# Splitting and joining the weights of an attention and MoE kernel another way, with an order read from a table

## The chip, the core and the metric

The kernel runs on one core of a Trainium2 chip. The metric is the device time of one execution in microseconds (us). The core has TensorE (PE in the profile; PEld is its weight loads), VectorE (DVE), ScalarE (ACT), GpSimd (POOL) and SyncE (SP), which here issues all the transfers. SBUF is the working memory; PSUM holds what TensorE writes, in banks of 128 x 512 float32.

## The reference, cut to what matters

```python
scores = scale * q @ k^T                 # 4 batches, 8 heads, 576 x 576, head size 64
mask   = scores >= 32nd largest of its row
attn   = softmax over the masked row;  x = attn @ v          # x: 2304 x 512
h = x @ w_in;  g = h * sigmoid(1.702 * h);  x = g @ w_out    # 512 -> 2048 -> 512
a = x @ w1;  b = x @ w2;  out = ((a * b) @ w3) @ w_out2      # 512 -> 1024 -> 1024 -> 512
```

The five weight matrices arrive as float64, q, k, v and x's path as float32. In the kernel w_out2 is called w4.

## The kernel before, in words

The 2304 rows are 18 tiles of 128. A tile runs through eight heads (`head`), `tile_end` (the 512 columns of x, scaled) and `moe`. A head is one score product `S` (L904, four matmuls of 288 columns; in tiles 4 and 13, which lie across two batches, eight), then on VectorE four MAX8 (L926) and three MATCH_REPLACE8 (L929) that find the 32nd largest of each row, then on ScalarE `cut` (L944), `exp` (L947) and `a hi` (L953), on GpSimd `a lo` (L956, L957), a DMA transpose, and for each pair of heads `av` (L971, 18 matmuls, or 36).

Every float32 factor of a product is cut into two float16 halves, hi and lo, and a product of 512 columns is three matmuls for each block of 128 rows (L668, L669, L670: hi by hi, hi by lo, lo by hi). `product_op` issues it as two operations of six matmuls, called half products here. A tile's `moe` has 28 of them: 8 `h`, 8 `x2`, 4 `a`, 4 `b` and 4 `o`, 504 in all; 32 more multiply w3 by w4 once (`w34`).

The weights are 72 blocks of 128 x 512: 8 of w4, 16 each of w3, w_in, w_out and of w1 and w2 together (`w12`). Each block goes through `load64`: a DMA of 512 KB into a raw buffer; `w low` on ScalarE (L513) and `w sign` on GpSimd or ScalarE (L518, L523), which put parts of the float32 word into the block; `w main` on ScalarE (L527), which rewrites the high words in the raw buffer; and `w join` on VectorE (L531), which joins the raw buffer's words to the block and frees the raw buffer. `l2_scale` then sums squares (`gram` on TensorE, L558) and works out one power-of-two scale `sc` for each matrix. `split_pe` makes the halves of a block: a float32 product with the identity brings it into a PSUM bank (`w in`, L595, two matmul records), ScalarE writes hi from the bank (`w hi`, L598), and VectorE writes lo as bank times scale less hi (`w lo`, L601). All 72 blocks go this way.

The four banks called `mm` serve all of these products; two larger pairs (`sp`) hold scores.

The order of the instructions on each engine is made before anything runs. The class `Order` holds every operation with the engines that may run it (`alts`), what it depends on and which buffers it takes (`acq`) and frees (`rel`); `run` goes forward in its own clock and gives each free engine, of the operations that could go, the one of least `prio`. In the kernel before, `prio` is a due time plus a shift that `later` reads from a table by the operation's name and due time, and where more than one engine may run an operation, the first that is free takes it, with waits from `LONGER`. The engines then run their lists strictly in order, and wait for each other by semaphores.

Of the kernel before, what the change touches and what calls it, by code (L numbers as in the profile page):

```python
# [19 lines left out]
P = 128  # L20
# [11 lines left out]
class Op:  # L32
    __slots__ = ("alts", "fn", "prio", "acq", "rel", "left", "users", "ready", "end", "eng", "lat", "tag", "seq", "done", "start", "why", "data")


class Order:
# [8 lines left out]
    def __init__(self):  # L45
        self.ops = []
        self.pools = {}
        self.both = set()

# [9 lines left out]
    def op(self, alts, due, deps=(), env=None, acq=(), rel=(), tag="", lat=None, data=0.6):  # L59
# [15 lines left out]
    def run(self, log=None):  # L75
# [13 lines left out]
        while n < len(self.ops):  # L89
# [18 lines left out]
            for e in engs:  # L108
# [65 lines left out]
PEP = ("w4", "w3", "win", "wout", "w12")  # L174
# [4 lines left out]
TIMES = (-20, 60, 130, 220, 330, 500, 750, 1000)  # L179
LATER = {  # L180
# [12 lines left out]
    'cut': (-16.5, -12.5, -10, 2.5, 54.5, -57, -110, -124),  # L193
    'diag': (36.5, -1.5, -37.5, -60, -103.5, -26, -28, -5.5),
    'diag sum': (77, 52, 49.5, 66, 118, 98, 82.5, 95),
    'esc': (-38.5, -52.5, -90.5, -104, -69, -58.5, -19.5, -46.5),
    'exp': (7, 5.5, -23.5, -30, -30, -23, 28, 80.5),
# [4 lines left out]
    'gram': (-18.5, 62.5, 143, 136, 220.5, 192.5, 75.5, 27),  # L202
# [72 lines left out]
}  # L275

def later(tag, due):

    v = LATER.get(tag)
    if v is None:  # L280
# [1019 lines left out]
```

## Time and profile before

| | |
|---|---|
| three runs, us | 1081.84, 1083.23, 1085.87 |
| median of the runs | 1083.23 us |
| span of the profiled execution, first to last instruction | 1081.3 us |
| TensorE busy | 990.1 us, 92% |
| VectorE busy | 932.2 us, 86% |
| ScalarE, GpSimd busy | 821.4 us (76%), 768.7 us (71%) |
| mean granted TensorE clock | 0.96 |

For the profiled execution only the span is given, no time of its own around it; the median lies 1.9 us above it. Busy is the time in which at least one instruction of the engine runs, so neighbours that overlap count once. A matmul's recorded length is longer than its turn on the engine: what a matmul costs in a full row is the distance from its start to the next start.

### The profile page before, as it was taken

The numbers are of one execution on the slowest core, as the hardware profiler recorded it, in microseconds if no ns is written. First come the engines' busy times: TensorE is split into PE (matmuls) and PEld (weight loads), VectorE is DVE, ScalarE is ACT, GpSimd is POOL, SyncE is SP. The second block draws the span as 40 slices with busy tenths as digits, with TensorE's granted clock in tenths as the row PEclk, the third lists the DMA queues.
The fourth block names the chain that finished last, engine by engine and source line by source line (L and its number), as shares of the span: only waits on it lengthen the run. The fifth ranks groups of instructions, "written<-read, shape, count | busy, mean of one in ns | idle before, by whom it ended". The sixth has DMA issues, their size and how long they took to land.

```text
span 1081.3 us, 18734 instructions
## 1 busy us (share of the span) xinstructions
PE 990.1 (92%) x5816; PEld 508.2 (47%) x5816; DVE 932.2 (86%) x2098; ACT 821.4 (76%) x1570; POOL 768.7 (71%) x1096
## 2 busy tenths in 40 slices
PE   4658899588899989999999998999999999999997
PEld 2334444334444445455454554555455555555443
DVE  4889899799999899999999999999999999996111
ACT  7878779888876778879788787778887887767432
POOL 4555545847757879879889878869799797767321
PEclk7779999699999999999999999999999999999999
DMA  8979968869836847876868858867877876556222
GB/s 254 287 200 244 236 128 251 161 149 199 175 73 104 147 104 151 141 143 123 146 126 151 148 110 134 157 129 120 145 135 120 144 141 123 103 111 119 48 59 68
DMA packets 428739, 156.96 MB, mean 145 GB/s; under 512 B 406624, under 2 KB 414816, under 8 KB 428640
## 3 DMA queue, kind: packets, MB, share of 16 engines
q1 hardware_dynamic: 428640, 155.78, 71.1%
q8 instruction: 45, 0.74, 0.3%
q14 instruction: 54, 0.44, 0.1%
HBM read 52.43 MB, written 4.72 MB: 53 GB/s over the span
## 4 chain that ended last, share of the span: by engine, by line
PE 50%; DVE 16%; DMA 11%; POOL 10%; ACT 8%; issue 4%; SPq 0%; POOLq 0%; DVEq 0%; ACTq 0%
PE mm L668 13%; PE mm L669 13%; PE mm L670 13%; DVE m8s L926 6%; DVE wsb L929 5%; DMA tsb<-hsb 5%; PE mm L971 4%; PE s_ps L904 4%; POOL hlb L957 2%; POOL hsb L456 2%; PE mm L595 2%; DMA ats<-hlb 2%; DMA qts<-hsb 1%; DMA wout<-in_moe_w_in_dram 1%; DVE w L531 1%
## 5 line engine op out<-in xcount | busy, mean ns | idle before, releaser
L926 DVE MAX8 m8s<-wsb 128x8 f32<-128x576 f32 x432 | 323.7, 755 | 4.8
L929 DVE MATCH_REPLACE8 wsb<-m8s,wsb 128x576 f32<-128x576 f32 x288 | 214.1, 743 | 0.0
L957 POOL TENSOR_TENSOR hlb<-ysb,hlb 128x512 f16<-128x512 f32 x144 | 167.9, 1166 | 0.0
L668 PEld LDWEIGHTS <-tsb 128*128 128x128 f16 x1072 | 104.9, 98 | 133.1 <-DMA tsb<-hsb 21.5
L668 PE MATMUL mm<-w,tsb 128*128 128x512 f16 x432 | 163.9, 379 | 2.7 <-DMA tsb<-hsb 2.5
L670 PEld LDWEIGHTS <-tsb 128*128 128x128 f16 x1072 | 105.1, 98 | 127.2 <-issue 1.3
L670 PE MATMUL mm<-w,tsb 128*128 128x512 f16 x432 | 163.7, 379 | 0.0
L669 PE MATMUL mm<-w,tsb 128*128 128x512 f16 x432 | 163.7, 379 | 0.0
L669 PEld LDWEIGHTS <-tsb 128*128 128x128 f16 x1072 | 104.9, 98 | 111.3 <-issue 8.0
L668 PE MATMUL mm<-wout,tsb 128*128 128x512 f16 x352 | 133.6, 380 | 7.6 <-DMA tsb<-hsb 5.4
L944 ACT ACTIVATE s_ps<-s_ps,m8s 128x576 f32<-128x576 f32 x144 | 102.8, 714 | 42.2 <-DVE m8s L926 34.1
L670 PE MATMUL mm<-wout,tsb 128*128 128x512 f16 x352 | 133.6, 380 | 0.0
L669 PE MATMUL mm<-wout,tsb 128*128 128x512 f16 x352 | 133.6, 380 | 0.0
L947 ACT ACTIVATE ysb<-s_ps,nbs,asm 128x576 f32<-128x576 f32 x144 | 120.2, 835 | 10.3 <-DVE nbs L936 4.8
L926 DVE MAX8 m8s<-s_ps 128x8 f32<-128x576 f32 x144 | 109.1, 758 | 16.4 <-PE s_ps L904 14.9
L668 PE MATMUL mm<-win,tsb 128*128 128x512 f16 x288 | 110.2, 383 | 7.2 <-DMA tsb<-hsb 7.0
L904 PE MATMUL s_ps<-kts,qts 128*128 128x288 f16 (+1 forms) x640 | 99.6, 295 | 13.2 <-ACT ysb L947 12.1
L669 PE MATMUL mm<-win,tsb 128*128 128x512 f16 x288 | 110.1, 382 | 0.0
L670 PE MATMUL mm<-win,tsb 128*128 128x512 f16 x288 | 109.9, 382 | 0.0
L1120 POOL TENSOR_TENSOR fsb<-fsb 128x512 f32<-128x512 f32 x68 | 87.4, 1286 | 29.7 <-ACT fsb L1111 25.6
L929 DVE MATCH_REPLACE8 wsb<-m8s,s_ps 128x576 f32<-128x576 f32 x144 | 107.9, 749 | 0.0
L971 PE MATMUL mm<-v2s,ats 128*128 128x130 f16 (+1 forms) x1440 | 96.3, 225 | 10.5 <-DMA ats<-hlb 8.1
(171 smaller groups left out, 1875.8 us busy)
## 6 DMA issues: line engine op xcount, KB each, us to landing
w<-in_moe_w_dram SPq DMA_DIRECT2D x16, 512.0 KB, 6.9
wout<-in_moe_w_in_dram SPq DMA_DIRECT2D x16, 512.0 KB, 5.7
wout<-in_moe_w_out_dram SPq DMA_DIRECT2D x16, 512.0 KB, 4.7
qts<-qts SPq DMA_DIRECT2D x36, 128.0 KB, 2.5
out_dram<-fsb SPq DMA_DIRECT2D x18, 256.0 KB, 2.4
w<-in_moe_w_out_dram SPq DMA_DIRECT2D x8, 512.0 KB, 6.3
psb<-in_moe_w_dram SPq DMA_DIRECT2D x8, 512.0 KB, 5.3
tsb<-in_moe_w_dram SPq DMA_DIRECT2D x8, 512.0 KB, 4.1
```

What stands on the lines that cost most here:

```text
L456: nc.gpsimd.tensor_tensor(lo(), src(), hi(), op=ALU.subtract)
L668: nc.tensor.matmul(o, a[:, i, :], hi, start=(first and i == 0), stop=False)
L669: nc.tensor.matmul(o, a[:, i, :], lo, start=False, stop=False)
L670: nc.tensor.matmul(o, a[:, 4 + i, :], hi, start=False, stop=(last and i == 3))
L904: nc.tensor.matmul(E["sp"][r : r + n, i], qe[q_][:, h, r : r + n], kt[:, j, i * HS : (i + 1) * HS], start=k_ == 0, stop=k_ == 1,)
L926: nc.vector.max(out=E["m8"][:, 8 * i : 8 * i + 8], in_=E["sp"] if i == 0 else E["w"])
L929: nc.vector.match_replace(out=two(E["w"]) if i == 0 else E["w"], in_to_replace=E["m8"][:, 8 * i : 8 * i + 8], in_values=E["sp"] if i == 0 ...
L944: nc.scalar.activation(E["sp"], E["sp"], AF.Prelu, bias=E["m8"][:, TOPK - 1 : TOPK], scale=-1.0, alpha=1.0 / FAR)
L947: nc.scalar.activation(two(E["y"]), E["sp"], AF.Exp, bias=E["nb"], scale=nesc)
L957: nc.gpsimd.tensor_tensor(hl()[:, S + SR : 2 * S], E["y"][:, 0:SM], hl()[:, 0:SM], op=ALU.subtract)
L971: nc.tensor.matmul(heads_av()[r : r + n, j_], e["at"][:, i, r : r + n], v2[:, j_, blk, :], start=(i == 0), stop=(i == 8))
L1120: nc.gpsimd.tensor_tensor(E["f"], E["f"], E["f2"], op=ALU.mult)
```

## The change

- `w main` writes its result into a bank of `mm` and no longer into the raw buffer, which is free from then on; `w join` reads the bank.
- `l2_scale` can write a scaled identity, identity times minus `sc`, with GpSimd (`w turn`) into a quarter of a tile of `tsb`. It is written for w4, for w3, for w1 and for w2.
- For these 40 blocks `split_pe` is new: a float32 product with the scaled identity puts minus the scaled block into the bank; ScalarE writes hi, minus the bank; a product of the bfloat16 view of the identity with hi adds hi to the bank (`w less`); lo, minus the bank, is written by ScalarE (`A`) or VectorE (`V`).
- For the 32 blocks of w_in and w_out `split_back` takes its place: ScalarE writes hi from SBUF; a product of the bfloat16 identity with hi puts hi into a bank (`w back`); VectorE writes lo, block times scale less bank.
- `prio` and the engine of every operation come from a table, `PLAN`. It unpacks to one word for each of the 5232 operations, in the order in which the code creates them: the low 13 bits are a rank (each of 0 to 5231 stands once), the high bits the number of the engine in `alts`. `TIMES`, `LATER`, `LONGER` and `later` are gone.
- An operation may be held back until another one has gone in the order (`after`): the loads of k, and of v, one after the other, likewise `k T`, `a hi`, `a T`, and `x T` behind the last `g T` of two tiles before. The buffer of k's transpose is taken at the load, that of x at the first `av`. These say what `run` may choose; no waits for the chip are written by them alone.

Counted through the code, the table's words say: of the 72 `w lo`, 32 are those of `split_back` on VectorE, 30 of the others stand on ScalarE and 10 on VectorE; `w sign` stands 60 times on GpSimd and 12 times on ScalarE. The operations of rank 0 to 2070 hold, among others, all 72 blocks' joins and splits, all 32 `w34`, 47 `S` (heads 0 to 46 in order), 185 MAX8, 139 MATCH_REPLACE8, 20 `av` and 91 half products of `moe`. Outside the weights the lo and hi operations of these ranks that VectorE has are: 10 `kv lo`, 8 of them those of the first batch, which are VectorE's in both kernels, 3 `q lo`, one of them likewise, 3 `p lo`, 3 `g lo`, 8 `kvr lo`, 5 `kvr hi`, and 6 other hi; ScalarE has 12 of the `w sign`. The operations behind the last MAX8 (rank 5068) hold 50 half products.

```diff
-        o.alts, o.prio, o.lat, o.data = alts, due + later(tag, due), lat, data
-        if len(alts) > 1:
-            o.alts = [(e, c, f, max(w + LONGER.get((tag, e), 0.0), -1.0)) for e, c, f, w in alts]
+        o.after = after
+        rank, k = self.plan[len(self.ops)]
+        o.alts, o.prio, o.lat, o.data = [(*alts[k][:3], 0.0)], 0.2 * rank, lat, data
...
-                    if o.done or r > now:
+                    if o.done or r > now or (o.after is not None and not o.after.done):
...
+def plan():
+    words = array.array("H", zlib.decompress(base64.b85decode("".join(PLAN))))
+    return [(w & 8191, w >> 13) for w in words]
...
         def f_main():
-            high = words(E[raw_pool])
-            nc.scalar.activation(high, high, AF.Copy, scale=2.0 ** -112)
+            nc.scalar.activation(E["mm"], words(E[raw_pool]), AF.Copy, scale=2.0 ** -112)
 
         def f_join():
             d = dst.bitcast(U32)
             nc.vector.scalar_tensor_tensor(
-                d, words(E[raw_pool]).bitcast(U32), 3, d, op0=ALU.logical_shift_left, op1=ALU.bitwise_or
+                d, E["mm"].bitcast(U32), 3, d, op0=ALU.logical_shift_left, op1=ALU.bitwise_or
             )
...
-        mn = act(0.57, due, f_main, deps=[ld, sg], tag="w main")
-        return dve(0.65, due, od.two(f_join), deps=[sg, mn], env=E, rel=[raw_pool], tag="w join")
+        mn = act(0.57, due, f_main, deps=[ld, sg], env=E, acq=["mm"], rel=[raw_pool], tag="w main")
+        return dve(0.62, due, f_join, deps=[sg, mn], env=E, rel=["mm"], tag="w join")
...
+        def f_turn():
+            nc.gpsimd.tensor_scalar(turned, ident, sc, -1.0, op0=ALU.mult, op1=ALU.mult)
...
+    def split_back(hi, lo, src, sc, due, deps, env=None, acq=()):
...
+        def f_hi():
+            nc.scalar.activation(hi(), src(), AF.Copy, scale=sc)
+
+        def f_back():
+            nc.tensor.matmul(E["mm"], upper(ident), hi(), start=True, stop=True)
+
+        def f_lo():
+            nc.vector.scalar_tensor_tensor(lo(), src(), sc, E["mm"], op0=ALU.mult, op1=ALU.subtract)
...
+    def split_pe(hi, lo, src, scaled, due, deps, env=None, acq=()):
...
         def f_in():
-            nc.tensor.matmul(E["mm"], ident, src(), start=True, stop=True)
+            nc.tensor.matmul(E["mm"], turned, src(), start=True, stop=False, skip_group_check=True)
 
         def f_hi():
-            nc.scalar.activation(hi(), E["mm"], AF.Copy, scale=sc)
+            nc.scalar.activation(hi(), E["mm"], AF.Copy, scale=-1.0)
+
+        def f_less():
+            nc.tensor.matmul(E["mm"], upper(ident), hi(), start=False, stop=True, skip_group_check=True)
 
         def f_lo():
-            nc.vector.scalar_tensor_tensor(lo(), E["mm"], sc, hi(), op0=ALU.mult, op1=ALU.subtract)
...
+            nc.scalar.activation(lo(), E["mm"], AF.Copy, scale=-1.0)
+
+        def f_lo_v():
+            nc.vector.tensor_scalar(lo(), E["mm"], -1.0, None, op0=ALU.mult)
...
-        hi = act(0.58, due + 6, f_hi, deps=[y], env=E, acq=["hl"], tag="a hi")
+        hi = act(0.58, due + 6, f_hi, deps=[y], env=E, acq=["hl"], tag="a hi", after=last_of.get("a hi"))
```

## Rows read from the trace of the kernel before

**Rows 1.** Stretches: from:to, length, busy by engine, clock, DMA share, GB/s.

```profile
40.00:80.00 40.00, 23.84 (x111) 12.59 (x112) 35.61 (x83) 30.67 (x64) 20.31 (x34) 0.75 0.89 218
...
200.00:240.00 40.00, 27.79 (x131) 14.02 (x130) 37.02 (x75) 31.64 (x57) 20.83 (x29) 0.79 0.70 145
...
0.00:400.00 400.00, 323.23 (x1765) 162.46 (x1766) 354.33 (x759) 312.39 (x578) 243.79 (x365) 0.90 0.80 183
400.00:440.00 40.00, 37.92 (x248) 19.90 (x247) 38.24 (x92) 30.30 (x61) 35.69 (x53) 0.96 0.72 136
440.00:960.00 520.00, 513.56 (x3215) 270.96 (x3213) 499.22 (x1157) 422.64 (x827) 440.52 (x617) 1.00 0.73 134
960.00:1081.30 121.30, 115.39 (x594) 54.93 (x592) 40.46 (x93) 56.06 (x105) 48.67 (x63) 1.00 0.38 74
```

**Rows 2.** The chain that ended last: start, length, what; a float32 product.

```profile
143.48 0.86 PE mm L595 x2
```

**Rows 3.** Timeline, TensorE: start, length, engine, line, operation.

```profile
955.51 0.65 PE L904 MATMUL s_ps<-kts,qts 128*128 128x288 f16 x4
...
956.00 1.21 PE L971 MATMUL mm<-v2s,ats 128*128 128x130 f16 x18
...
957.05 0.38 PE L668 MATMUL mm<-w,tsb 128*128 128x512 f16 x1
...
957.27 0.38 PE L669 MATMUL mm<-w,tsb 128*128 128x512 f16 x1
```

**Rows 4.** TensorE's groups by line, 0 to 400 us: count, busy, mean ns, idle before.

```profile
L668 PE MATMUL mm<-wout,tsb 128*128 128x512 f16 x112 | 42.6, 380 | 6.3 <-DMA tsb<-hsb 4.1 <-DVE w L726 0.8 <-DVE hsb L601 0.6
L904 PE MATMUL s_ps<-kts,qts 128*128 128x288 f16 x140 | 26.8, 321 | 10.5 <-ACT ysb L947 9.5 <-DMA qts<-qts 0.8
L971 PE MATMUL mm<-v2s,ats 128*128 128x130 f16 x288 | 24.0, 241 | 8.3 <-DMA ats<-hlb 6.1 <-DVE w L726 1.4 <-DVE w L601 0.3
L668 PE MATMUL mm<-w,tsb 128*128 128x512 f16 x62 | 23.6, 380 | 0.2 <-DVE w L601 0.2
...
L668 PE MATMUL mm<-win,tsb 128*128 128x512 f16 x52 | 20.2, 388 | 4.5 <-DMA tsb<-hsb 4.5
...
L904 PE MATMUL s_ps<-kts,qts 128*64 128x288 f16 x64 | 5.7, 291 | 1.4 <-ACT ysb L947 1.4
L971 PE MATMUL mm<-v2s,ats 128*64 128x130 f16 x108 | 5.3, 228 | 0.0
```

**Rows 5.** Timeline, VectorE: the distance between starts; the last MAX8.

```profile
960.27 0.74 DVE L926 MAX8 m8s<-wsb 128x8 f32<-128x576 f32 x1
...
960.93 0.07 DVE L929 MATCH_VALUE_LOAD wsb<-m8s,s_ps 128x8 f32 x1
...
961.65 0.09 DVE L929 MATCH_VALUE_LOAD wsb<-m8s,wsb 128x8 f32 x1
...
990.07 0.76 DVE L926 MAX8 m8s<-wsb 128x8 f32<-128x576 f32 x1
```

**Rows 6.** VectorE's groups by line, 0 to 400 us.

```profile
L926 DVE MAX8 m8s<-wsb 128x8 f32<-128x576 f32 x127 | 94.8, 752 | 0.7
...
L926 DVE MAX8 m8s<-s_ps 128x8 f32<-128x576 f32 x43 | 32.6, 758 | 6.0 <-PE s_ps L904 5.2 <-ACT w L523 0.5
...
L531 DVE SCALAR_TENSOR_TENSOR w<-wout,w 128x512 uint32<-128x512 uint32 x32 | 26.5, 844 | 4.4 <-ACT wout L527 4.3
L601 DVE SCALAR_TENSOR_TENSOR wout<-mm,wsm,wout 128x512 f16<-128x512 f32 x24 | 17.4, 743 | 0.3
...
L726 DVE SCALAR_TENSOR_TENSOR w<-mm,w 128x512 f16<-128x512 f32 x8 | 5.5, 682 | 2.3 <-ACT w L723 2.3
```

**Rows 7.** All of L531 (joins) in one stretch, busy us.

```profile
sum 360.00, DVE 61.19; mean DVE 6.80
```

**Rows 8.** ScalarE's groups by line, 0 to 400 us: a read from a bank.

```profile
L598 ACT ACTIVATE wout<-mm,wsm 128x512 f16<-128x512 f32 x24 | 16.3, 685 | 5.3 <-PE mm L595 5.3
```

**Rows 9.** TensorE's waits, 0 to 400 us: for whom, us, times, longest.

```profile
PE s_ps L904 <- ACT ysb L947: 10.9, 8, 3.6
```

More of the change, by code (lines that the diff above doesn't have):

```diff
@@ L1 @@
+import array
+import base64
 import heapq
+import zlib
 from contextlib import ExitStack
@@ L32 @@
 class Op:
-    __slots__ = ("alts", "fn", "prio", "acq", "rel", "left", "users", "ready", "end", "eng", "lat", "tag", "seq", "done", "start", "why", "data")
+    __slots__ = ("alts", "fn", "prio", "acq", "rel", "left", "users", "ready", "end", "eng", "lat", "tag", "seq", "done", "start", "why", "data", "after")
 class Order:
@@ L173 @@
 PE_DUE, PE_OUT = 100.0, 20.0
[L174 removed]
+TURN = ("w4", "w3")
 SIGN_G = 0.5
[L179 to L180 removed]
[12 rows of a table removed]
[L193 to L197, printed above, removed]
[4 rows of a table removed]
[L202 removed]
[12 rows of a table removed]
[L215 removed]
[19 rows of a table removed]
[L235 to L238 removed]
[27 rows of a table removed]
[L266 removed]
@@ L545, in wcol, with l2_scale @@
         return wsm[:, ncol[0] - 1 : ncol[0]]
-    def l2_scale(blocks, deps):
+    def l2_scale(blocks, deps, turned=None, free=()):
         E = {}
@@ L587, in l2_scale @@
         c = dve_chain(due, f_scale, deps=[b], env=E, rel=["mm"], tag="w scale")
-        return inv, sc, c
-    def split_pe(hi, lo, src, sc, due, deps, env=None, acq=()):
+        if turned is None:
+            return inv, sc, c
+        return inv, (turned, pool(0.35, due - 40, f_turn, deps=[c] + list(free), tag="w turn")), c
+    def split_back(hi, lo, src, sc, due, deps, env=None, acq=()):
         E = {} if env is None else env
+        def f_hi():
[4 more added lines that the diff above has]
+            nc.vector.scalar_tensor_tensor(lo(), src(), sc, E["mm"], op0=ALU.mult, op1=ALU.subtract)
+        h = act(0.61, due - PE_OUT, f_hi, deps=deps, env=E, acq=acq, tag="w hi")
+        b = pe(0.24, due - PE_DUE, f_back, deps=[h], env=E, acq=["mm"], tag="w back")
+        return dve(0.66, due - PE_OUT, f_lo, deps=[b], env=E, rel=["mm"], tag="w lo")
@@ L600, in f_lo @@
         def f_lo():
-            nc.vector.scalar_tensor_tensor(lo(), E["mm"], sc, hi(), op0=ALU.mult, op1=ALU.subtract)
-        a = pe(0.87, due - PE_DUE, f_in, deps=deps, env=E, acq=["mm"] + list(acq), tag="w in")
-        h = act(0.58, due - PE_OUT, f_hi, deps=[a], tag="w hi")
-        return dve(0.66, due - PE_OUT, f_lo, deps=[h], env=E, rel=["mm"], tag="w lo")
-    def split_all(w, first, srcs, sc, deps, name):
-        if name not in PEP:
-            return [split_to(w, first + i, src, sc, deps) for i, src in enumerate(srcs)]
+            nc.scalar.activation(lo(), E["mm"], AF.Copy, scale=-1.0)
@@ new lines, in f_lo_v, with split_all @@
+        def f_lo_v():
+            nc.vector.tensor_scalar(lo(), E["mm"], -1.0, None, op0=ALU.mult)
+        a = pe(0.87, due - PE_DUE, f_in, deps=list(deps) + [ready_turned], env=E, acq=["mm"] + list(acq), tag="w in")
+        h = act(0.48, due - PE_OUT, f_hi, deps=[a], env=E, tag="w hi")
+        l = pe(0.24, due - PE_DUE, f_less, deps=[h], env=E, tag="w less")
+        return op([("A", 0.48, f_lo, 0.0), ("V", 0.6, f_lo_v, 1.0)], due - PE_OUT, deps=[l], env=E, rel=["mm"], tag="w lo")
+    def split_all(w, first, srcs, scaled, deps):
@@ L729, in weights @@
             ready["w34"].append(dve(0.66, due, f_lo34, deps=[h34], env=E, rel=["mm"], tag="w34 lo"))
-        ii, si, di = l2_scale([block(w12, i) for i in range(16)], cin)
-        ready["win"] = split_all(win, 0, [block(w12, i) for i in range(16)], si, [di] + sp3, "win")
+        ii, si, di = l2_scale([block(w12, i) for i in range(16)], cin, quarter(4, 2) if "win" in TURN else None)
+        ready["win"] = split_all(win, 0, [block(w12, i) for i in range(16)], si, [di] + sp3)
         cout = [
@@ L734, in weights @@
         ]
-        io, so, do = l2_scale([block(w12, i) for i in range(16)], cout)
-        ready["wout"] = split_all(wout, 0, [block(w12, i) for i in range(16)], so, [do] + cout + pr, "wout")
+        io, so, do = l2_scale([block(w12, i) for i in range(16)], cout, quarter(4, 3) if "wout" in TURN else None)
+        ready["wout"] = split_all(wout, 0, [block(w12, i) for i in range(16)], so, [do] + cout + pr)
         srcs = [rows(w, i, j) for w in (w1, w2) for j in range(NP_) for i in range(KB)]
@@ L818, in f_sum @@
             nc.tensor.matmul(E["mm"][:, 0:1], ones[0:SR], upper(ar)[0:SR], start=False, stop=True)
-        ld = dma(2.1 if is_v else 1.5, due - 6, f_load, env=E, acq=[sk, "rest"] + (["v2"] if is_v else ["h", "kr"]), tag="kv load", data=1.0)
+        ld = dma(
+            2.1 if is_v else 1.5, due - 6, f_load, env=E, acq=[sk, "rest"] + (["v2"] if is_v else ["h", "kr", "kt"]), tag="kv load",
+            data=1.0, after=last_of.get(("load", is_v)),
+        )
+        last_of["load", is_v] = ld
         a = act(0.93, due, f_abs, deps=[ld], tag="kv abs")
@@ L840, in f_t @@
             nc.sync.dma_start_transpose(out=E["kt"][:, :, SM:S], in_=E["kr"].rearrange("p h d -> p (h d)"))
-        kready[b, hp] = [dma(3.9, due, f_t, deps=[m, r], env=E, acq=["kt"], rel=["h", "kr"], tag="k T", data=1.1)]
+        last_of["k T"] = dma(
+            3.9, due, f_t, deps=[m, r], env=E, rel=["h", "kr"], tag="k T", data=1.1, after=last_of.get("k T")
+        )
+        kready[b, hp] = [last_of["k T"]]
     qready, qhold = {}, {}
@@ L1070, in tile_end @@
         )
-        X["xt"] = dma(1.32, due, f_t, deps=[s], env=X, acq=["t"], rel=["h"], tag="x T")
+        X["xt"] = dma(1.32, due, f_t, deps=[s], env=X, acq=["t"], rel=["h"], tag="x T", after=last_of.get(("g T", t - 2)))
     def hi_lo(due, E, src, deps, rel, acq=(), tag="", wait=2.0, wait_hi=2.0):
```

190 lines of the change are left out of this document (125 added, 65 removed), and 80 rows, old and new, of tables (LATER, LONGER).

## The prediction

> **What bounds the kernel now.** I read the stretches first, then the two timelines, then the groups by line, then the waits. The stretches cut the span in two. From 440 to 960 us TensorE is busy 513.6 of 520 us at a clock of 1.00, and from 960 to the end 115.4 of 121.3; before 400 us it is busy only 323.2 of 400, at a mean clock of 0.90 [rows 1]. So from 400 us on the end is set by how much TensorE work is still to be done, and before that TensorE has room. There VectorE is the fullest engine, 354.3 of 400 us, with ScalarE next, 312.4 [rows 1]; VectorE stays full, 499.2 of 520 us from 440 to 960, until its last MAX8 ends at 990.8, 90.5 us before the end [rows 1, 5]. A reader should take from this that a microsecond of TensorE work saved before 400 us is worth nothing by itself. It counts only if products of later stages move forward into the room, and these wait for VectorE: for the weights' joins and splits and for the heads.
>
> **TensorE's account of the kernel before.** A product matmul takes 0.216 us from start to start (957.05 to 957.27), so a half product of six takes 1.295; a score matmul 0.122 (955.51 to 956.00, four of them); an `av` matmul 0.058 (956.00 to 957.05, eighteen) [rows 3]. By 400 us 112 + 62 + 52 = 226 first lines L668 had run, two in each half product [rows 4]: 113 half products, 32 of them `w34`, so 81 of 504. Scores: 140 + 64 = 204 of 640. `av`: 288 + 108 = 396 of 1440 [rows 4]. Left: 423 x 1.295 = 547.8, 436 x 0.122 = 53.2, 1044 x 0.0583 = 60.9, and some 5 for the k and v sums: 666.9 us. Idle time after 400 us by the stretches: 2.1 + 6.4 + 5.9 = 14.4 [rows 1]. The sum, 681.3, is what lies between 400 us and the end of the span. The account closes, so I use it for the kernel after.
>
> **The change part by part.**
>
> *TensorE's weights.* A float32 product of 512 columns takes 0.86 us [rows 2]; 72 make 61.9. After: 40 x 0.86 = 34.4, and 72 products with the bfloat16 identity. None with that mix of types is in the trace; the nearest row is the 16-bit matmul, 0.216, the far end the float32 product, 0.86. I take 0.22: 15.8. Saved: 11.7 us (at the far end 34 us more than before). All of it lies before 400 us, where TensorE idles, so it is costed at nothing by itself.
>
> *VectorE's joins.* 72 joins took 61.2 us [rows 7], 0.85 each, while two-input operations that read a bank take 0.68 (L726) to 0.74 (L601) [rows 6]. I take 0.71: 10 us saved, 8 to 12 at the ends. [...]
>
> *VectorE's lo.* 40 of the 72 leave L601, 0.74 recorded and some 0.65 from start to start, as MAX8 is 0.75 recorded and 0.66 apart [rows 5, 6]. 30 go to ScalarE: 19.5 us saved; 10 stay as a one-input operation, about the same.
>
> *What VectorE takes on.* By the table's ranks up to 2070, ten more lo of 512 columns x 0.65 = 6.5, six hi at about half = 2, thirteen small `kvr` operations at 0.1 to 0.6, say 0.25, = 3.3: 12 us.
>
> So by rank 2070 VectorE is relieved of 10 + 19.5 - 12 = 17.5 us. A head costs it 4 x 0.66 + 3 x 0.72 = 4.8 us [rows 5], so that is 3.6 heads. The table agrees with this: it has 185 MAX8 and 139 MATCH_REPLACE8 by that rank, where the kernel before had 127 + 43 = 170 and 127 by 400 us [rows 6], and 15 x 0.66 + 12 x 0.72 = 18.5 us. VectorE's work up to rank 2070 is therefore that of the kernel before up to 400 us, within 1 us. If VectorE is held up as much as before, rank 2070 is reached at 400 us.
>
> *ScalarE.* It takes 30 lo at 0.57 from start to start (0.69 recorded from a bank [rows 8], less the same overlap) = 17; 11 more `w sign` x 0.66 = 7; for 3.75 more heads and 10 more half products about 18. That is 312.4 + 42 = 354 of 400 us: as full as VectorE. This is not hidden, and it is what the rivals rest on.
>
> *The rest.* Four `w turn` on GpSimd, under 0.5 us each, stand before the first split of their matrix; GpSimd is busy 243.8 of 400 [rows 1]. The raw buffer comes free one join earlier, but a bank is held from `w main` to `w join`: at 0.7 for each of the two and as much for the waits between, an estimate, 2 us x 72 = 144 of 1600 bank-us up to 400. SP issues the same transfers; `after` and the earlier `acq` change the order that was chosen, and their effect is within the table's. A new wait is that of `w less` and `w back` for ScalarE's hi: behind it on TensorE stand scores, `av` and half products of other tiles, and VectorE waits for the scores. I cost it at nothing because TensorE has 113 us of room before 400 us; without that cover each microsecond counts fully.
>
> **The sum.** At rank 2070 the table has done 91 half products, 47 heads' scores (32 x 4 + 8 x 8 + 7 x 4 = 220 matmuls) and 20 `av` (16 x 18 + 4 x 36 = 432). Left: 413 x 1.295 = 534.8, 420 x 0.122 = 51.2, 1008 x 0.0583 = 58.8, and 5: 649.8 against 666.9. That is 17.1 us less to do from 400 us on. Is TensorE still the bound there? VectorE has 97.75 heads x 4.8 = 469 us left, and about 75 for the rest of its work up to the last MAX8; at the 96% of 440 to 960 us [rows 1] this takes 567, to 967 us, and the 50 half products behind it take 65, so its own floor is some 1042 with the last tile's latencies. TensorE is later, and bounds. With the idle time of before the span is 1081.3 - 17.1 = 1064.2; the median of the runs lies 1.9 above the span of the profiled execution, so **1066 us**.
>
> **The rivals.**
>
> *A better filled start.* VectorE stands idle 45.7 us before 400 us [rows 1]. An order with a rank for each operation may close half of this, and TensorE has room to follow. Then rank 2070 comes 20 us earlier: 1046, near VectorE's floor of 1042, which is as far as this goes. For: the old order knew only a name and a time. Against: the idle time is spread, 4.4 us from 40 to 80 and 3.0 from 200 to 240 [rows 1], and some is that of the first loads.
>
> *Nothing comes of it.* VectorE's 17.5 us turn into waits for a ScalarE that is now as full as it is: 1083.
>
> *TensorE waits for ScalarE (slower).* Its list is strict, so a `w less` or `w back` whose hi is late holds up the scores behind it, and VectorE with them. TensorE already waited for ScalarE's exp eight times before 400 us, 10.9 us in all, 1.4 each, 3.6 at most [rows 9]. With 72 new such places, 0.24 us of delay to VectorE at each take back the 17 us: that is the point from which it decides. At half the length of the waits seen, 0.7, but only two places in three, it is 33 us: 1066 + 33 = 1099.
>
> [...]
>
> **How the numbers follow.** The forecast has 0.46 (1055 to 1077 by its unknown costs), the better start 0.22, nothing 0.12, the slower one 0.14, the clock 0.06. Half a per cent, 5.4 us, is about what a measurement can tell here. Faster: 0.46 + 0.22 and a little of the clock's, 0.69. Within: 0.12 and most of the clock's, 0.17. Slower: 0.14. The range takes in the better start down to VectorE's floor and the slower rival's nearer half: 1040 to 1090.
>
> **What would show it.** Right: by 400 us some 185 MAX8 and 91 half products of `moe`; VectorE busy near 354 us there; `w join` recorded at 0.68 to 0.74; bfloat16 identity products 0.22 us apart; TensorE full from 400 us on; the last MAX8 some 65 to 75 us before the end instead of 90.5. Wrong: idle TensorE rows of `w less` or `w back` behind ScalarE that add up to more than 17 us with idle MAX8 behind scores; a clock under 0.85 between 120 and 320 us; TensorE with idle time of over 20 us after 400.

## The result and the profile after

| | before | after |
|---|---|---|
| median of four runs each, us | 1084.55 (1081.84 to 1086.64) | 1066.2 (1064.11 to 1068.41) |
| ratio after to before | | 0.984, 95% interval 0.982 to 0.986 |
| span of the profiled execution, us | 1081.3 | 1066.6 |
| last MAX8 starts at, us | 990.1 | 993.4 |
| from there to the end of the span, us | 91.2 | 73.2 |
| by 400 us: MAX8, half products of `moe` | 170, 81 | 180, 86 |

The median is the predicted time, 1066. The way there is not the predicted one in full, and that is what the rest is about. The profiled execution of the kernel after is the longest of its four, 1068.4 us, so the two spans lie 14.7 us apart where the medians lie 18.4.

The stretches of the kernel after, with the columns of [rows 1] (from:to, length, busy time of TensorE, its weight loads, VectorE, ScalarE and GpSimd, granted clock, DMA share, GB/s):

```profile
0.00:400.00 400.00, 317.66 (x1816) 163.63 (x1816) 346.76 (x789) 327.90 (x618) 222.79 (x355) 0.88 0.80 185
400.00:440.00 40.00, 39.37 (x262) 21.25 (x261) 37.70 (x86) 32.63 (x66) 32.03 (x42) 1.00 0.86 157
440.00:960.00 520.00, 515.39 (x3221) 272.05 (x3220) 501.13 (x1157) 399.38 (x780) 424.69 (x611) 1.00 0.70 131
960.00:1066.60 106.60, 101.18 (x530) 48.61 (x527) 48.06 (x98) 50.44 (x94) 39.55 (x55) 1.00 0.42 82
...
200.00:240.00 40.00, 25.18 (x138) 14.27 (x138) 35.48 (x76) 34.99 (x62) 24.57 (x34) 0.66 0.81 176
...
280.00:320.00 40.00, 33.32 (x185) 16.12 (x183) 32.76 (x77) 30.97 (x54) 26.65 (x40) 0.91 0.69 144
320.00:360.00 40.00, 40.00 (x277) 20.52 (x276) 35.52 (x86) 34.17 (x73) 26.93 (x52) 1.00 0.55 106
360.00:400.00 40.00, 40.00 (x227) 19.67 (x224) 37.34 (x85) 27.09 (x53) 26.12 (x39) 1.00 0.58 105
```

From 400 us on TensorE is as full as before, with 0.6 + 4.6 + 5.4 = 10.6 us idle against 14.4 [rows 1]. It is full earlier, though: 40.0 of 40 us in both slices from 320 to 400 us, where the kernel before had 39.6 and 34.2. VectorE did not reach the predicted 354 us busy by 400 us, but 346.8, less than before. ScalarE went up to 327.9, not 354.

The groups of TensorE from 0 to 400 us (count, busy, mean ns, idle before), which answer to [rows 4]:

```profile
L669 PE MATMUL mm<-wout,tsb 128*128 128x512 f16 x114 | 44.5, 390 | 9.9 <-DMA tsb<-hsb 9.8
...
L903 PE MATMUL s_ps<-kts,qts 128*128 128x288 f16 x152 | 28.2, 313 | 11.0 <-ACT ysb L946 8.7 <-DMA qts<-qts 2.2
L669 PE MATMUL mm<-w,tsb 128*128 128x512 f16 x64 | 24.3, 380 | 0.0
...
L669 PE MATMUL mm<-win,tsb 128*128 128x512 f16 x58 | 22.7, 392 | 5.3 <-DMA tsb<-hsb 2.6 <-DVE w L537 1.1 <-DVE wout L612 0.8
...
L903 PE MATMUL s_ps<-kts,qts 128*64 128x288 f16 x64 | 5.5, 292 | 0.0
```

They hold (114 + 64 + 58) / 2 = 118 half products, 32 of them `w34`, so 86 of `moe`, and 216 score matmuls; `av` stands at 396 matmuls as before. By the prediction's account 418 x 1.295 + 424 x 0.122 + 1044 x 0.0583 + 5 = 658.9 us are left at 400 us, against 666.9. With 10.6 idle this is 669.5 where the span leaves 666.6, so the account is 2.9 too long here. The 14.7 us of the two spans are therefore 8.0 of less work left at 400 us, 3.8 of less idle time after it, and 2.9 that the account doesn't place.

The groups of VectorE, 0 to 400 us, which answer to [rows 6, 7], and the last MAX8 (one line's view: shortest, median and longest ns, first and last start), which answers to [rows 5]:

```profile
L925 DVE MAX8 m8s<-wsb 128x8 f32<-128x576 f32 x134 | 99.4, 751 | 0.5
...
L925 DVE MAX8 m8s<-s_ps 128x8 f32<-128x576 f32 x46 | 34.9, 760 | 11.7 <-PE s_ps L903 9.4 <-ACT xsb L1011 0.7 <-ACT hlb L952 0.5
...
L537 DVE SCALAR_TENSOR_TENSOR w<-mm,w 128x512 uint32<-128x512 uint32 x48 | 32.4, 680 | 8.5 <-ACT mm L533 6.4 <-POOL nbs L935 2.0
...
L537 DVE SCALAR_TENSOR_TENSOR win<-mm,win 128x512 uint32<-128x512 uint32 x16 | 10.7, 682 | 1.2 <-ACT mm L533 1.1
...
L537 DVE SCALAR_TENSOR_TENSOR wout<-mm,wout 128x512 uint32<-128x512 uint32 x8 | 5.4, 689 | 3.7 <-ACT mm L533 3.5
```

```profile
L925 DVE MAX8 m8s<-wsb x17: 734/761/762, 960.7 to 993.4; 128x8 f32<-128x576 f32 x17
```

The 72 joins take 48.5 us instead of 61.2. The last head is through 3.3 us later than before, and what stands behind it is 18.0 us shorter, which at 1.295 is the work of 14 half products.

### The profile page after: what moved, and what is told of

It is laid out like the page before. It is cut to its first block, busy times and chain, and to the rows that moved or that the text cites. A ratio compares the mean times of both kernels' runs of the same rounds, so it can differ in the third digit from the quotient of the medians.

```text
span 1066.6 us, 18717 instructions
## 1 busy us (share of the span) xinstructions
PE 973.6 (91%) x5824; PEld 505.5 (47%) x5824; DVE 933.6 (88%) x2127; ACT 810.3 (76%) x1556; POOL 719.1 (67%) x1060
## 4 chain that ended last, share of the span: by engine, by line
PE 52%; DVE 14%; DMA 11%; ACT 8%; POOL 8%; issue 5%; SPq 2%; POOLq 0%; ACTq 0%; DVEq 0%
PE mm L669 13%; PE mm L671 13%; PE mm L670 13%; DVE m8s L925 6%; DVE wsb L928 5%; PE mm L970 5%; DMA tsb<-hsb 4%; PE s_ps L903 4%; PE mm L624 2%; DMA wout<-in_moe_w_in_dram 1%; POOL hlb L956 1%; POOL hsb L463 1%; DVE win L612 1%; POOL fsb L1119 1%; ACT ysb L946 1%
## 5 line engine op out<-in xcount | busy, mean ns | idle before, releaser
L952 ACT CAST hlb<-ysb 128x576 f16<-128x576 f32 x144 | 97.2, 675 | 13.1 <-DMA ats<-hlb 12.1
L955 POOL TENSOR_TENSOR hlb<-ysb,hlb 128x64 f16<-128x64 f32 x144 | 44.5, 309 | 90.1 <-ACT hlb L952 88.5
```

The source lines that it names most:

```text
L952: nc.scalar.copy(hl()[:, 0:S], E["y"])
L955: nc.gpsimd.tensor_tensor(hl()[:, S : S + SR], E["y"][:, SM:S], hl()[:, SM:S], op=ALU.subtract)
```

## The experiments

Times are medians in us; "more than after" is against 1066.2. The kernel before measured 1083.1 to 1084.6 beside them; the kernel after was not run again, so a difference from it holds to a microsecond or two.

| kernel | us | ratio to before (95%) | more than after | last MAX8 starts | from there to the end |
|---|---|---|---|---|---|
| before | 1084.6 |  |  | 990.1 | 91.2 |
| after | 1066.2 | 0.982 to 0.986 | 0 | 993.4 | 73.2 |
| old forms, new table | 1113.3 | 1.025 to 1.029 | 47 | 1038.2 | 73.3 |
| new forms, old rule of order | 1144.2 | 1.052 to 1.058 | 78 | 1053.2 | 87.7 |
| joins undone | 1098.1 | 1.011 to 1.017 | 32 | 1028.4 | 73.7 |
| splits undone | 1109.0 | 1.021 to 1.026 | 43 | 1033.2 | 73.5 |
| one planned latency 3.0 for 2.8 | 1102.8 | 1.014 to 1.020 | 37 | 1032.7 | 73.3 |
| raw buffer freed late in the planning | 1131.5 | 1.042 to 1.047 | 65 | 1053.5 | 73.2 |
| the same lists, join from SBUF | 1145.6 | 1.052 to 1.059 | 79 | 1070.2 | 73.4 |
| lo of w_in and w_out twice (VectorE) | 1090.8 | 1.005 to 1.009 | 24.6 | 1016.1 | 73.2 |
| hi of w_in and w_out twice (ScalarE) | 1093.8 | 1.007 to 1.011 | 27.6 | 1019.2 | 73.2 |
| their product in float32 (TensorE) | 1080.7 | 0.996 to 0.999 | 14.5 | 1004.9 | 75.4 |
| MAX8 twice in 32 heads (VectorE) | 1078.5 | 0.994 to 0.997 | 12.3 | 1004.1 | 73.2 |
| 12 signs moved to GpSimd | 1063.9 | 0.981 to 0.985 | -2.3 | 988.7 | 73.2 |

The last two columns are of the profiled executions. In all twelve kernels that have the table's ranks, 73 to 75 us lie behind the last MAX8, whatever was done to them; in the two that have the old rule it is 88 and 91. So the shorter end is the table's doing. And whatever a kernel loses or gains otherwise, it loses or gains before the last head.

**Undoing the change by halves.** First the old instructions in the order that the table's ranks give, and the new instructions with the old rule for the order (what an operation waits for in the planning, and where it takes its buffers, as after):

```diff
 # old forms, new table: the joins and splits of the kernel before,
 # each operation with the rank that the table gives its successor
-        rank, k = self.plan[len(self.ops)]
+        rank, k = self.plan[self.at]
 # new forms, old rule
-        rank, k = self.plan[len(self.ops)]
-        o.alts, o.prio, o.lat, o.data = [(*alts[k][:3], 0.0)], 0.2 * rank, lat, data
+        o.alts, o.prio, o.lat, o.data = alts, due + later(tag, due), lat, data
```

> The order of the changed kernel (the rank of every operation, the engine of all but the splits' lo) with the instructions of the kernel before: joins read the raw buffer, all 72 splits go by a float32 product with the identity and VectorE's lo. Theory of relief (the gain is VectorE's work before 400 us, taken away by the new instructions): VectorE gets back about 12.7 us of joins and 19.5 us of lo, with no order that was made for it, so rank 2070 comes some 30 us later: 1085 to 1100. Theory of order (the gain is the rank for each operation): 1066 to 1072. Theory of TensorE (the gain is the 12 us of float32 products): 1076 to 1080.

> The instructions of the changed kernel with the order of the kernel before: due times, the shifts and waits of the old tables, the engine that is free first; the operations that are new have no shift, and the holds and the earlier taking of buffers of the change stay. Theory of relief: most of the gain stays, 1066 to 1074, since 17 us of VectorE's work are gone whatever the order. Theory of order: the gain is gone, 1083 or more, and old tables that were made for other instructions may make it worse, to 1095.

Measured 1113.3 and 1144.2, both above every range that was named. Either half alone is slower than both whole kernels. The table brings nothing without the instructions that it was made for. The new instructions bring nothing under the old rule; but its shifts were made for the old instructions, and no run has the new ones with shifts made for them.

**Undoing one part.** The joins alone (main writes back into the raw buffer, the join reads and frees it), and the splits alone (72 float32 products, hi and lo as before):

```diff
-            nc.scalar.activation(E["mm"], words(E[raw_pool]), AF.Copy, scale=2.0 ** -112)
+            high = words(E[raw_pool])
+            nc.scalar.activation(high, high, AF.Copy, scale=2.0 ** -112)
...
-        mn = act(0.57, due, f_main, deps=[ld, sg], env=E, acq=["mm"], rel=[raw_pool], tag="w main")
-        return dve(0.62, due, f_join, deps=[sg, mn], env=E, rel=["mm"], tag="w join")
+        mn = act(0.57, due, f_main, deps=[ld, sg], tag="w main")
+        return dve(0.65, due, od.two(f_join), deps=[sg, mn], env=E, rel=[raw_pool], tag="w join")
```

> The changed kernel with the joins alone undone: main writes into the raw buffer, join reads it and frees it, no bank is taken. Theory of relief: joins go back from 0.68 to about 0.85 us, 12.7 us of VectorE's work before 400 us, 1074 to 1079. Theory of order: 1066 to 1069. Theory of TensorE: 1066.

> The changed kernel with the splits alone undone: 72 float32 products with the identity, hi on ScalarE from the bank, all lo on VectorE, no scaled identity. Theory of relief: VectorE gets back 30 lo at 0.65, 19.5 us, and ScalarE loses 17: 1078 to 1086. Theory of order: 1066 to 1070. Theory of TensorE: 12 us more on TensorE before 400 us, 1076 to 1079, with VectorE's count of MAX8 by 400 us unchanged at 180.

Measured 1098.1 and 1109.0, again above every range: 32 and 43 us more than after, which together is four times the whole gain. Read as prices of the parts this makes no sense. The next run shows why.

**A change with nothing in it.** This run was the last one made. The instructions, ranks, engines, buffers and their release are those of the kernel after; the planner alone is told that a load of a weights' block takes 3.0 us and not 2.8:

```diff
-        ld = dma(0.5, due - 20, f_load, deps=deps, env=E, acq=[raw_pool], tag="w load", lat=2.8, data=1.8)
+        ld = dma(0.5, due - 20, f_load, deps=deps, env=E, acq=[raw_pool], tag="w load", lat=3.0, data=1.8)
```

> The kernel after with one number of the planning changed: the latency that the planner assumes for the load of a weights' block, 3.0 us instead of 2.8. Instructions, ranks, engines, buffers and the points where they are freed are all those of the kernel after; only the order that comes out of the planning differs, from the first splits on. Theory A, the table's order is robust, and what undoing a part cost came from the instructions and the buffer: within 5 us of the kernel after, 1061 to 1071. Theory B, the ranks are fitted to the planner's durations, and any deviation costs tens of microseconds whatever its content: 1085 to 1135; then most of what undoing the joins (32 us), the splits (43 us) or the raw buffer's release (65 us) cost is no price of theirs. Between, 1071 to 1085, the misfit explains a part of each.

Measured 1102.8, 37 us more. The profile of this kernel, 0 to 400 us, its stretch and the groups of half products and scores:

```profile
0.00:400.00 400.00, 304.22 (x1668) 155.43 (x1669) 327.82 (x731) 310.84 (x588) 207.10 (x332) 0.86 0.78 179
```

```profile
L669 PE MATMUL mm<-wout,tsb 128*128 128x512 f16 x112 | 45.9, 410 | 6.7 <-DMA tsb<-hsb 4.7 <-DVE w L537 2.0
L903 PE MATMUL s_ps<-kts,qts 128*128 128x288 f16 x136 | 25.5, 316 | 17.8 <-ACT ysb L946 16.1 <-DMA qts<-qts 1.4
L669 PE MATMUL mm<-win,tsb 128*128 128x512 f16 x58 | 22.7, 391 | 2.2 <-DMA tsb<-hsb 1.4 <-DVE wout L612 0.4 <-DVE win L612 0.3
L669 PE MATMUL mm<-w,tsb 128*128 128x512 f16 x35 | 14.5, 414 | 1.0 <-DMA tsb<-hsb 1.0
```

All engines do less by 400 us; the half products of `moe` are (112 + 58 + 35) / 2 - 32 = 70.5 instead of 86, and TensorE waits 16.1 us for ScalarE's exp instead of 8.7. So the ranks give their order only in the planner's clock for which they were made, and a deviation without content costs as much as undoing a part. What undoing a part cost is then no price of that part: 37 us of misfit hide any price of ten. One run gives the size of one misfit only, so it can't be subtracted from another. This is theory B of that run, and it takes the meaning, as prices, from the three runs above that have the table's ranks.

**What a microsecond costs, with all lists kept.** Here an operation is issued twice in its place, or made longer, and each engine's list is otherwise that of the kernel after. On VectorE and ScalarE, and on TensorE (where the bank gets the block and not hi, so lo of w_in and w_out holds other values):

```diff
 # lo twice: split_back's f_lo issues its instruction twice; hi twice: its f_hi
 # float32 product
-            nc.tensor.matmul(E["mm"], upper(ident), hi(), start=True, stop=True)
+            nc.tensor.matmul(E["mm"], ident, src(), start=True, stop=True)
```

> The changed kernel, every engine's list in the same order, with each of the 32 lo of w_in and w_out on VectorE issued twice: 32 x 0.66 = 21 us more of VectorE's work before 400 us. Theory of relief (VectorE's time before 400 us sets how far products move forward, about one for one): 1066 + 21 = 1083 to 1089, with 4 fewer heads by 400 us. Rival, slack (ScalarE or the raw buffers set the pace, and VectorE's work is hidden): 1066 to 1072. Rival, fitted lists (anything that departs from the times for which the order was made costs a multiple of itself): 1100 or more.

> The same order, with each of the 32 hi of w_in and w_out on ScalarE issued twice: 32 x 0.64 = 20.5 us more of ScalarE's work before 400 us, where it is busy 328 us. Theory of relief with VectorE alone in the lead: 1066 to 1074. Rival, ScalarE sets the pace as much as VectorE: 1082 to 1088. Rival, fitted lists: 1100 or more.

> The same order, with the 32 bfloat16 products of w_in and w_out done as float32 products of the block: 32 x 0.64 = 20.5 us more of TensorE's work before 400 us (the lo that it leaves is not the reference's, since the bank holds the block without its scale). Theory of relief (TensorE has room before 400 us): 1066 to 1070. Theory of TensorE (its work counts one for one): 1084 to 1088. Rival, fitted lists: 1090 or more.

Measured: 24.6, 27.6 and 14.5 us more than after. The first two lie somewhat above the ranges in which their engine leads, the third lies between its theories. What was added is more than the expectations say. A second lo does not overlap the first as other neighbours do: in the timeline of VectorE a pair takes 1.44 us from its start to the next operation's, and one lo of the kernel after 0.66. The first two rows are of the kernel with lo twice, the others of the kernel after:

```profile
178.46 1.52 DVE L612 SCALAR_TENSOR_TENSOR win<-w,wsm,mm 128x512 f16<-128x512 f32 x2
179.90 0.75 DVE L925 MAX8 m8s<-wsb 128x8 f32<-128x576 f32 x1
```

```profile
174.43 0.74 DVE L612 SCALAR_TENSOR_TENSOR win<-w,wsm,mm 128x512 f16<-128x512 f32 x1
175.09 0.76 DVE L925 MAX8 m8s<-wsb 128x8 f32<-128x576 f32 x1
```

That is 32 x 0.78 = 25 us on VectorE, so 1.0 for each one added. On ScalarE a pair takes 1.37 where one takes 0.62, so 24 us were added and each cost 1.15. On TensorE it is 32 x (0.86 - 0.22) = 20.5, 0.7 for each. The stretches from 0 to 400 us of the three, in this order:

```profile
0.00:400.00 400.00, 301.83 (x1685) 153.61 (x1686) 349.25 (x774) 315.16 (x593) 209.28 (x334) 0.87 0.77 179
```

```profile
0.00:400.00 400.00, 300.80 (x1667) 153.50 (x1668) 323.81 (x733) 333.62 (x620) 208.29 (x332) 0.89 0.77 179
```

```profile
0.00:400.00 400.00, 322.82 (x1796) 167.63 (x1797) 338.61 (x765) 322.21 (x609) 215.09 (x342) 0.89 0.78 183
```

In each the engine that got the work is a little fuller than after, or as full, and the others do less; in the second VectorE is busy only 323.8 us instead of 346.8. Half products of `moe` by 400 us: 72.5, 70.5 and 79. By the prediction's steps the time on TensorE should have cost nothing and that on VectorE one for one. VectorE's came out so, TensorE's did not. At these places none of the three has room that could be given away, though in the kernel after VectorE, ScalarE and TensorE idle for 53, 72 and 82 us before 400 us. All three additions lie on the weights' way from block to product, which they also make longer; for ScalarE and TensorE no run tells the engine's time from the length of that way.

The lo operations lie close together on the way from the blocks to the products. In the next kernel the same time goes to VectorE in another place, the fourth MAX8 of the first 32 heads:

```diff
-            nc.vector.max(out=E["m8"][:, 8 * i : 8 * i + 8], in_=E["sp"] if i == 0 else E["w"])
+            ...  # the same, and once more for i == 3 in tiles 0 to 3
```

> The kernel after with the fourth MAX8 of each of the first 32 heads issued twice, with every engine's list otherwise as it was: 32 x 0.66 = 21 us more VectorE work before 400 us, on the heads' chain and not on the weights' chain. Theory A, engine time on VectorE is what counts before 400 us: the same as with the lo operations issued twice, +20 to +28 us on the kernel after, 1086 to 1094. Theory B, what counted there was the length of the chain by which the weights become ready: this chain is left alone here, VectorE has about 50 us of idle time before 400 us, and less than half of the added time is seen, 1070 to 1077. By 400 us A expects some 165 to 168 MAX8 of the old count and under 75 half products; B over 80 half products.

Measured 1078.5: 12.3 us for some 25 (a pair takes 1.46 us to the next start, one MAX8 0.68), 0.5 for one, half of what the same time costs in the splits. By 400 us 44 heads had begun (46 after, 42 with lo twice), and there were (112 + 56 + 51) / 2 - 32 = 77.5 half products. It lies between the two theories: VectorE's time counted in both places, and about twice as much on the weights' way. The lo lie between 170 and 270 us and these MAX8 begin at 36, so the moment may have its part in that.

**Relief.** The 12 signs that ScalarE has go to GpSimd, in the same places:

```diff
-        sg = op([("A", 0.63, f_sign_a, 0.0), ("G", 0.75, f_sign, SIGN_G)], due, deps=[lo], tag="w sign")
+        sg = op([("A", 0.63, f_sign, 0.0), ("G", 0.75, f_sign, SIGN_G)], due, deps=[lo], tag="w sign")
```

> The kernel after with the 12 sign operations of ScalarE moved to GpSimd, at the same place in the order of creation and rank: some 8 us less for ScalarE and 9 us more for GpSimd before 400 us, nothing else changed. Theory A, ScalarE's time counts as fully as VectorE's before 400 us (1.35 us for each added one): 8 to 11 us faster than the kernel after, 1055 to 1058. Theory B, added time counts but relief does not, since each list was fitted to the durations it had: 1063 to 1069. Theory C, the 12 signs on ScalarE stand where GpSimd was the later one: the raw words wait for GpSimd, and it is slower than the kernel after, 1070 to 1080.

Measured 1063.9, ratio 0.981 to 0.985 where the kernel after has 0.982 to 0.986: the same within the noise, and in the range of theory B. 8 us more on ScalarE would cost 9 by the rate above; 8 less brought 2.3, and the intervals leave room for no gain and for one of about 5. The profiled executions differ more: by 400 us this one has 138 + 46 = 184 MAX8 and (116 + 64 + 62) / 2 - 32 = 89 half products, and its span is 1061.9 us. So the relief was seen to count for less than load, and not shown to count for nothing.

**The raw buffer, and the join's own price.** First the planning frees the raw buffer at the join instead of at main, with all instructions as after; then, with the lists of that kernel, main writes back into the raw buffer and the join reads it there:

```diff
 # freed late
-        mn = act(0.57, due, f_main, deps=[ld, sg], env=E, acq=["mm"], rel=[raw_pool], tag="w main")
-        return dve(0.62, due, f_join, deps=[sg, mn], env=E, rel=["mm"], tag="w join")
+        mn = act(0.57, due, f_main, deps=[ld, sg], env=E, acq=["mm"], tag="w main")
+        return dve(0.62, due, f_join, deps=[sg, mn], env=E, rel=["mm", raw_pool], tag="w join")
 # and, for the second kernel, f_main and f_join on words(E[raw_pool])
```

> The kernel after, its ranks and engines as they were, but in the planning the raw buffer is freed by the join and no longer by the main step; the join still reads the bank. The instructions and their costs are those of the kernel after; only the loads of the raw words start one join later and the order that follows from it differs. Theory A, the earlier release costs and brings nothing, as the prediction put it: 1062 to 1072. Theory B, the earlier release of the raw buffer carries a part of the gain (loads start later, grams and products wait for them): 1080 to 1095. In B idle time before grams behind joins grows to over 15 us before 400 us.

> As the kernel with the raw buffer freed by the join, with the very same lists, but the main step writes its result back into the raw buffer and the join reads it there, as in the kernel before. Against that kernel this is the cost of the instructions alone: joins 0.83 to 0.85 instead of 0.68, 11 to 12 us more VectorE work on the weights' chain. Theory A, VectorE's time before 400 us counts 1.17 for one: 12 to 15 us more than that kernel. Theory B, the whole of what undoing the joins cost (32 us) comes from the instructions: 25 to 32 us more. Theory C, it comes from the release and the order: 0 to 5 us more.

Measured 1131.5 and 1145.6. The first is 65 us over the kernel after, outside both ranges, but that contains a misfit of unknown size, 37 in the run above; TensorE's wait for grams behind joins is not what grew (21.0 us in all, after 23.9). What the earlier release is worth stays open. The second differs from the first in the join's and main's operands alone, and that is a price: 14.1 us by the medians, 12 with some 5 either way by the means. The joins of the two, first from the bank, then from SBUF, in the view of one line (shortest, median, longest ns):

```profile
L537 DVE SCALAR_TENSOR_TENSOR w<-mm,w x48: 670/680/692, 90.2 to 319.2; 128x512 uint32<-128x512 uint32 x48
```

```profile
L537 DVE SCALAR_TENSOR_TENSOR w<-wout,w x32: 666/800/1697, 91.5 to 234.9; 128x512 uint32<-128x512 uint32 x32
```

Summed over their groups all 72 joins take 48.7 us in the first and 62.9 in the second, and `w main` on ScalarE and `w sign` on GpSimd take some 2 us more each. 14.2 us of VectorE, with these, are worth 14.1: theory A, about one for one, in a kernel that is 65 us slower than after.

## Why the prediction was right, and where it was not

**The sum came out, one of its terms did not.** It had 17.1 us less TensorE work left at 400 us and the idle time of before. There were 8.0 us less work and 3.8 less idle time, and 2.9 that the account doesn't place. That the number is met to 0.2 us is luck: the profiled span came 2.4 us above the forecast 1064.2, and the median lies 2.2 below that execution. The step that failed is "rank 2070 is reached at 400 us": it was reached later, with 180 MAX8 and 86 half products where 185 and 91 were named.

**The same gain over the whole span.** TensorE's busy time in the kernel before is 990.1 us, so it idles 91.2. The first row of the page of the kernel after, and that of the kernel whose 32 products went back to float32:

```profile
PE 973.6 (91%) x5824; PEld 505.5 (47%) x5824; DVE 933.6 (88%) x2127; ACT 810.3 (76%) x1556; POOL 719.1 (67%) x1060
```

```profile
PE 989.7 (92%) x5856; PEld 514.5 (48%) x5856; DVE 936.1 (87%) x2127; ACT 809.8 (75%) x1556; POOL 721.0 (67%) x1060
```

After, TensorE is busy 16.5 us less and idles 93.0, 1.8 more. The forecast, 17.1 us less with 11.7 less work, meant 5.4 us less idle time. With the float32 products put back TensorE is busy 989.7 and idles 90.6 of 1080.3 us, nearly the kernel before, though joins, lo and table are those of the kernel after. So work taken from TensorE is a rival for much of the gain that the runs don't refute. They don't prove it either: without the heads that came forward, 180 MAX8 by 400 us for 170, the idle time need not have stayed the same.

**Why it came later.** The step set VectorE's work against VectorE's room "if VectorE is held up as much as before". It was held up more: 53.2 us idle by 400 us against 45.7. Most of the difference lies in one slice: from 280 to 320 us VectorE was busy 32.8 of 40 us, before 38.9; the other slices differ by up to 2.5 us either way and nearly cancel. The largest wait of VectorE there (total, times, longest), then rows of its timeline and ScalarE's:

```profile
DVE w L537 <- ACT mm L533: 5.3, 2, 3.1
```

```profile
292.63 0.69 DVE L537 SCALAR_TENSOR_TENSOR w<-mm,w 128x512 uint32<-128x512 uint32 x1 [3.11 <-ACT mm L533]
```

```profile
288.39 0.69 ACT L1107 ACTIVATE fsb<-mm,msm 128x512 f32<-128x512 f32 x1 [3.08 <-PE mm L671]
...
291.87 0.66 ACT L533 ACTIVATE mm<-psb 128x512 f32<-128x512 f32 x1
```

The join waits for main, and main stands in ScalarE's list behind an activation of `moe` (L1107) that waited 3.1 us for TensorE's product. The load is not what main waited for: `w low` of the same block began at 290.16 without a wait. The product was late for two reasons that rows show: TensorE stood idle for most of the 4 us before (its last wait there, 2.6 us, was for a transpose), and then ran at a granted clock of 0.57, with its matmuls 0.43 us apart from 284.50 to 287.49 and 0.22 from 288.36 on:

```profile
280.00:284.00 4.00, 1.33 (x15) 0.85 (x13) 4.00 (x15) 3.58 (x7) 2.06 (x4) 1.00 1.10 247
284.00:288.00 4.00, 4.00 (x12) 1.49 (x11) 3.97 (x9) 0.81 (x2) 3.81 (x6) 0.57 1.09 249
```

The second wait, 2.2 us at 306.2, is of the same kind: its main stands behind a ScalarE operation of `moe` that waited 2.4 us for a transpose. So ScalarE, held up by `moe` in its strict order, held up VectorE.

The new place of release made main, not the join, the step behind which loads queue; over 0 to 400 us SyncE's queue waits 37.6 us for it, where it had waited 19.4 for joins, as the first row of that view shows for before and then for after:

```profile
SPq L508 <- DVE w L531: 19.4, 14, 4.2
```

```profile
SPq L515 <- ACT mm L533: 37.6, 19, 9.0
```

With every releaser that the view names, the loads waited 38.8 us before and 44.7 after, so most of that rise is a change of name. "Comes free one join earlier" was costed at nothing; its price, if it has one, is not settled.

**"Worth nothing by itself" is not borne out.** The prediction gave TensorE's 11.7 us of float32 products no value, since TensorE idles before 400 us. Adding 20.5 us there cost 14.5. The idle time lies before 320 us and the products that are added lie at 170 to 260 us, in the same stretch in which the weights are made and waited for; from 320 us TensorE is full. The saved 11.7 may then have brought up to 8 us, at the rate of 0.7, but relief on ScalarE was seen to count less than load, so this is an estimate, from that rate alone, and no share that a run shows.

**VectorE was not the one lead.** The prediction let it lead before 400 us and had ScalarE as a threat. A microsecond added to ScalarE cost 1.15, to VectorE 0.5 to 1.0. That they lead in turn, each waiting for the other, fits this and the waits above; relieving one alone (the signs) brought nothing clear of the noise.

**Terms.** The joins: 10 us expected, 12.7 measured, because a join from a bank takes 0.68 and not 0.71; and one microsecond of it was worth about one where it could be priced (14.1 for 14.2). The bfloat16 identity product, 0.22 taken between 0.216 and 0.86, stands 0.21 to its next in a full row of the timeline of TensorE, kernel after:

```profile
128.33 0.38 PE L630 MATMUL mm<-hsb,ident 128*128 128x512 f16 x1
128.54 0.65 PE L903 MATMUL s_ps<-kts,qts 128*128 128x288 f16 x4
```

ScalarE's addition was put too high: 15.5 us came, not 42. Fewer heads and half products were done than the forecast had, the 40 hi from a bank cost 0.60 instead of 0.69, and main 0.64 instead of 0.66 to 0.68. And some 9 us of small hi left ScalarE (that line's groups sum to 17.1 us before and 8.1 after); the prediction charged VectorE for what it takes on of these and did not take it from ScalarE.

**The rivals.** The better filled start did not come: VectorE idles more, not less. "Nothing comes of it" named what happened in part: VectorE's relief turned into waits for ScalarE. No run shows the term behind the 0.06 that the forecast gives the clock; in its place the runs showed a clock of 0.66 from 200 to 240 us, where it had been 0.79, and of 0.57 in the 4 us above, and from 120 to 320 us a mean of 0.91 (before 0.93), above the bound of 0.85. "TensorE waits for ScalarE" exists, but is small. TensorE's waits from 0 to 400 us, kernel after:

```profile
PE mm L564 <- DVE w L537: 12.2, 4, 5.1
PE s_ps L903 <- ACT ysb L946: 8.7, 7, 2.7
PE mm L564 <- DVE wout L537: 7.9, 1, 7.9
PE mm L630 <- ACT hsb L627: 5.2, 3, 3.7
...
PE mm L630 <- ACT wout L627: 1.9, 3, 0.9
...
PE mm L609 <- ACT wout L606: 1.0, 1, 1.0
```

The three rows of `w less` and `w back` make 8.1 us in seven places of 72, less than the 17 from which it would have decided; the wait for exp is shorter than in [rows 9], 8.7 against 10.9.

**What stays open.** Which share of the gain belongs to the joins, to VectorE's lo, to TensorE's shorter products and to the order. The runs that undo one part can't say, since the order was no longer that of the table. With the old rule and its old shifts the new instructions are slower than the kernel before, so some new order was needed; that it had to be this table is not shown. The 18.0 us less behind the last head are the table's doing, but it can only put these half products earlier where there is room for them. That the joins and splits give the room is argued; how much each gives, no run here can tell.

## What to carry to other kernels

An idle engine is no proof that its time is free: issue one of its operations twice in place, with all else kept, and read what a microsecond costs there before an edit is costed at nothing. Do it at the place that the edit touches, since the price on one engine differed by a factor of two between two places, and read from the timeline how much was added. An experiment on a kernel whose order was planned for its own durations must keep the lists; one run that changes the order and nothing else tells how large a misfit can be. Load and relief are two measurements: here what was added to an engine was seen each time, and the one thing that was removed from one was not, beyond the noise.

## What the runs showed of the hardware

**A join out of a bank was not held up by GpSimd.** The joins of the kernel before, in the view of one line, and those of the kernel after:

```profile
L531 DVE SCALAR_TENSOR_TENSOR w<-wout,w x32: 676/685/1768, 87.2 to 210.9; 128x512 uint32<-128x512 uint32 x32
...
L531 DVE SCALAR_TENSOR_TENSOR wout<-w,wout x8: 680/1006/1239, 11.8 to 30.1; 128x512 uint32<-128x512 uint32 x8
```

```profile
L537 DVE SCALAR_TENSOR_TENSOR w<-mm,w x48: 666/679/693, 92.1 to 306.2; 128x512 uint32<-128x512 uint32 x48
...
L537 DVE SCALAR_TENSOR_TENSOR wout<-mm,wout x8: 681/691/692, 11.7 to 28.2; 128x512 uint32<-128x512 uint32 x8
```

With both inputs in SBUF more than half of the joins took some 0.68, and the others up to 1.77; from a bank none took over 0.69. The long ones lie beside GpSimd's work: of the 54 joins that stand singly in the timeline of the kernel before, 23 took over 0.72, and all 23 overlap an instruction of GpSimd, as do 18 of the other 31, at 0.67 to 0.69; after, 43 of 60 overlap one, and none took over 0.69. A pair of the kernel before: GpSimd's sign begins at 104.85 and takes 0.78, a join that begins at 104.92 ends after 1.18.

```profile
104.85 0.78 POOL L518 TENSOR_SCALAR w<-wout 128x512 bf16<-128x512 f32 x1 [0.83 <-DMA wout<-in_moe_w_in_dram]
```

```profile
104.92 1.18 DVE L531 SCALAR_TENSOR_TENSOR w<-wout,w 128x512 uint32<-128x512 uint32 x1
```

GpSimd pays as well: the signs of its largest group took 0.865 each before (31 of them; of the 21 that stand singly, the six over 0.80, 0.95 to 1.22, all overlap a join) and 0.773 after (30), and in the two kernels with the same lists 0.80 with joins from SBUF against 0.77 from the bank. What decides which of the joins that overlap GpSimd become long is not shown. Reading a bank did not make the join dearer: the medians are 0.685 from SBUF and 0.679 from the bank.

**A scale given as a constant.** ScalarE's hi from a bank took 0.685 to 0.699 with a scale for each partition and 0.596 to 0.603 with the constant -1, for the same 128 x 512 ([rows 8] has a group before; one after):

```profile
L627 ACT ACTIVATE hsb<-mm 128x512 f16<-128x512 f32 x16 | 9.5, 596 | 3.7 <-PE mm L624 3.7
```

With the constant it took 82 to 103 ns less.
